# The front of batch 0 in pair order: first keys and queries issued first, small casts and x copies on ScalarE, the sine's table ahead of six of them

## The chip, the cores and the metric

One core of one Trainium2 chip runs the whole program. The metric is device time in microseconds (us), as a median over runs. A core has five engines, each with an instruction queue of its own that is worked through in order: TensorE (PE in the profile, its weight loads PEld), VectorE (DVE), ScalarE (ACT), GpSimd (POOL) and SyncE (SP), which here only issues DMAs. Sixteen DMA engines move data for whichever queue issued the transfer. An instruction that must wait for another engine or for a DMA waits on a semaphore, and everything behind it in its queue waits as well.

## The reference

Two parts in a row: attention in chunks of 32 queries over 56 keys around them and 8 memory keys, then a feed-forward layer with the "snake" activation.

```python
# q, k, v: 4 batches, 8 heads, 768 positions, 64 dims; mem_k, mem_v: 8 rows per head
for c in range(24):
    q_c = q[:, :, 32*c : 32*c+32]
    k_full = concat([mem_k, k[:, :, max(0, 32*c-16) : min(768, 32*c+40)]])
    v_full = concat([mem_v, v[:, :, the same rows]])
    scores = q_c @ k_full.T / 8
    a = exp(scores - max);  a = a / (sum(a) + 1e-9)
    out[:, :, 32*c : 32*c+32] = a @ v_full

x = out as 3072 tokens of 512            # heads side by side
h = x @ w_in                             # 512 x 2048
g = h + sin(alpha * h)**2 / (alpha + 1e-9)
result = g @ w_out                       # 2048 x 512, float32
```

## The kernel before

The kernel works through the four batches one after the other. Attention of a batch gives xT, the layer's input with its 512 columns on the partitions; the layer is then computed in 16 tiles of 128 hidden units ("b" and "h" are the two halves of a tile's first product, followed by the sine on ScalarE; "q" squares it, "g" finishes the tile) and a second product with w_out. While a batch's layer runs on TensorE, the attention of the next batch is worked in between. For batch 0 there is nothing to work it into: everything until the first tile's sine is the *front*, and it is the part that the change touches.

The order of the work is written out by hand. `WORDS` holds one string per stage; `Stage.run` takes it word by word, and a word such as `a4A` calls `do_a("4A")`, which issues the instructions. Each engine gets its instructions in the order of these words. The words of the front:

- `aNE` (L691, L693): casts float32 data to bf16; N is 0 to 3 for the keys of head pair 0 to 3 (k0 to k3), 4 to 7 for the queries (q0 to q3); E is the engine, V for VectorE, A for ScalarE. Pair 3 comes through GpSimd (`dq068`, `dk068`), whose DMAs cast.
- `kN`, `lN` (L313): TensorE turns keys or queries of pair N by 12 transposes. `KNE` (L324), `LNE` (L333): the engine E puts the turned keys into kT, the queries into qT.
- `sNH` (L351, L359, L366): mask and scores of pair N, half H, and their exponential on ScalarE. `vNH` (L378, L387, L388): product with the values on TensorE, then reciprocal and product on VectorE ("normalisation", out comes x_blk).
- `tNH`, `TNH` (L400, L403): TensorE transposes x_blk, and VectorE (t) or ScalarE (T) copies it into xT.
- `Ck` (L812 to L820): memory keys cast, turned and, by `put_memk` (L244), spread into kT of batch 0 and of batch 1. `Cf` (L827) casts the memory values, `m0` (L225) spreads them into vw. `Cl` makes alpha, `Cb`, `Cm`, `Ci` the mask.
- `p0`, `P0` (L462): the first three of the four terms of tile 0's halves, those of the pairs in EARLY. `We`, `Ws` (L743): a one-element activation that makes ScalarE load the table of exp or of sin.
- `yN`, `zN` (L730, L724): matmuls of zeros that keep TensorE busy. `V024` and its like: loads of values of batch 0 by GpSimd (heads 2 and 3 here). `dm`, `I02`, `I27`: memory values of the other batches and w_in by GpSimd.

The float loads of k and q (`load_f`, L753) are issued ahead of all words, keys on SP's queue, queries on ScalarE's own. The eight hardware semaphores DMAHW0 to DMAHW7 are given to these DMAs in turn; a DMA that takes a semaphore for the second time first waits until the earlier DMA on it has landed. PSUM has eight banks; scores, values and a tile take two, a turn or an x transpose takes one, and `Banks` hands them out as the program is built.

Of the kernel before, what the change touches and what calls it, by code (L numbers as in the profile page):

```python
# [11 lines left out]
NEG = -30000.0  # L12
CROSSED = {0: (0, 0), 1: (0, 0), 2: (1, 1), 3: (1, 1)}
KW = 1024
EARLY = (0, 1, 3)
BF = mybir.dt.bfloat16
F32 = mybir.dt.float32
ACTF = mybir.ActivationFunctionType
# [2 lines left out]

WORDS = (
    (
# [4 lines left out]
    ),  # L28
    (
# [93 lines left out]
def kernel(  # L123
# [12 lines left out]
    nc = tc.nc  # L136
    B, H, S, D = q.shape
    NM = mem_k.shape[2]
# [3 lines left out]
    HP = H // 2  # L142
# [31 lines left out]
    memv_st = consts.tile([P, B, H, D], BF, name="memv_st")  # L174
# [4 lines left out]
    NK = NM * sum(not CROSSED[b][0] for b in range(B))  # L179
    memk_bf = memv_st[0:NK, 0]  # L180
# [43 lines left out]
    def put_memv(b, eng=None):  # L224
        (eng or nc.vector.tensor_copy)(  # L225
            vws[b % 2][64:72, :, :, 0:D],
            memv_st[64:72, b, :, :].unsqueeze(2).to_broadcast([NM, H, NJ, D]),
        )

    def put_memv_heads(b):  # L230
        for h in range(H):
            nc.gpsimd.tensor_copy(
                vws[b % 2][64:72, h, :, 0:D],
                memv_st[64:72, b, h, :].unsqueeze(1).to_broadcast([NM, NJ, D]),
            )
# [7 lines left out]
    def put_memk(b):  # L243
        nc.vector.tensor_copy(  # L244
            kTs[b % 2][:, :, 24:856].rearrange("p g (j c) -> p g j c", c=104)[:, :, :, 40:40 + NM],
            memkT[:, :, NM * b:NM * b + NM].unsqueeze(2).to_broadcast([P, HP, NJ, NM]),
        )
# [208 lines left out]
    def half_tile(t, hf, kts=range(KT)):  # L456
        done = t["done"][hf]
        for kt in kts:
            if kt in done:
                continue  # L460
            done.append(kt)
            nc.tensor.matmul(  # L462
                t["hT"][:, hf, 0:HALF],
                w_in_sb[:, kt, P * t["ft"]:P * t["ft"] + P],
                t["xT"][:, kt, HALF * hf:HALF * hf + HALF],
                start=(len(done) == 1), stop=(len(done) == KT),
            )

    def opened(ft, xT):
        hT, bs = banks.pair()  # L470
        return {"ft": ft, "xT": xT, "hT": hT, "bs": bs, "done": [[], []]}
# [69 lines left out]
    class Stage:  # L541
# [29 lines left out]
        def early(self, a, hf):  # L571
            if int(a) not in self.tile:
                self.tile[int(a)] = opened(int(a), self.next_x() if self.i < 0 else self.xT)
            half_tile(self.tile[int(a)], hf, EARLY if self.i < 0 else range(3))

# [101 lines left out]
        def do_m(self, a):  # L677
            put_memv(int(a))

        def do_H(self, a):  # L680
            put_memv_heads(int(a))

# [64 lines left out]
    kq_f = [mlp.tile([P, 2, 6 * D], F32, name="kq_f", tag=t) for t in ("u", "s2") * 4]  # L747
    memk_f = mlp.tile([P, H, D], F32, name="memk_f", tag="o_sb", bufs=3)
    memv_f = mlp.tile([P, H, D], F32, name="memv_f", tag="o_sb", bufs=3)
    alpha_rows = mlp.tile([FT, P], F32, name="alpha_rows", tag="o_sb", bufs=3)  # L750

    def load_f(ring, src, hp, t):
        ring.dma_start(  # L753
            t[:], src[0, 2 * hp:2 * hp + 2].rearrange("h (p r) d -> p h (r d)", p=P)
        )

    for bb in range(B):
        if not CROSSED[bb][0]:
            nc.scalar.dma_start(memk_f[NM * bb:NM * bb + NM], mem_k[bb].rearrange("h n d -> n h d"))
    nc.sync.dma_start(alpha_rows[:], moe_alpha.rearrange("(ft p) -> ft p", p=P))  # L760
    for hp in range(HP - 1):
        load_f(nc.sync, k, hp, kq_f[hp])
        load_f(nc.scalar, q, hp, kq_f[4 + hp])
        if hp == 0:
            nc.sync.dma_start(memv_f[64:72], mem_v[0].rearrange("h n d -> n h d"))
    nc.vector.memset(zeros[:], 0.0)
    nc.vector.memset(tiny[:], 0.0)
    nc.vector.memset(mcol[:], 0.0)
# [33 lines left out]
    def const_i():  # L802
# [5 lines left out]
        nc.gpsimd.tensor_copy(mind[:, 0, 0, :], asum[:, 5:6].to_broadcast([P, 32]))  # L808
        nc.gpsimd.tensor_copy(mind[:, NJ - 1, 2, :], asum[:, 6:7].to_broadcast([P, 32]))

    def const_k():
        nc.vector.tensor_copy(memk_bf, memk_f[0:NK])  # L812
        bank, bs = banks.single()
        mt = bank[:, 0:2 * NK].bitcast(BF).rearrange("p (g c) -> p g c", g=HP)
        for g in range(HP):
            nc.tensor.transpose(
                mt[:, g, :], memk_bf[:, 2 * g:2 * g + 2, :].rearrange("p e d -> p (e d)"),
                ident[0:NK, 0:NK]
            )
        nc.vector.tensor_copy(memkT[:], mt)  # L820
        put_memk(0)
        if not CROSSED[1][0]:
            put_memk(1)
        banks.give(bs)

    def const_f():
        nc.vector.tensor_copy(memv_st[64:72, 0], memv_f[64:72])  # L827

    def const_l():
        nc.vector.tensor_copy(ident_f[:], ident[0:FT, 0:FT])  # L830
# [20 lines left out]
    def const_s():  # L851
        nc.gpsimd.memset(kst[0:32, 0, :], 0.0)
        nc.gpsimd.memset(kst[96:128, NJ - 1, :], 0.0)

    consts_of = dict(b=const_b, f=const_f, m=const_m, i=const_i, k=const_k, l=const_l, p=const_p, v=const_v,
                     s=const_s, z=const_z)

    first = {}
# [35 lines left out]
```

## Time and profile before

| what | us |
| --- | --- |
| median of 3 runs | 215.82 |
| lowest, highest run | 214.7, 217.43 |
| span of the profiled execution | 212.0 |
| TensorE busy in that span | 203.1 |
| VectorE, ScalarE, GpSimd busy | 139.9, 142.8, 100.8 |

The runs are timed from outside, the span runs from the first to the last instruction of one profiled execution; the median lies 3.8 above the span. The execution has no time of its own beside its span.

In the rows below, a timeline row is: start in us from the span's start, us taken, engine, source line, operation, out<-in with the shape, how many were merged, and in brackets the idle time before it with what ended it. A row of the chain of waits is start, us, and what held the chain. ACTq and SPq are the issuing of DMAs by those queues. A row of the windows view is a stretch, its length, the busy time (and count) of PE, PEld, DVE, ACT and POOL, the granted TensorE clock, the mean share of the DMA engines, and GB/s.

### The profile page before, as it was taken

What the parts mean: (1) busy time and instruction counts of PE and PEld (TensorE: products, weight loads), DVE (VectorE), ACT (ScalarE), POOL (GpSimd) and SP (SyncE); (2) the same over time, 40 slices, a digit from 0 to 9 for tenths busy, and PEclk for the clock granted to TensorE, in tenths of its full rate; (3) what the DMA queues carried; (4) which work ended last, traced back from release to release, by engine and by line L of the source; (5) the groups of instructions that cost most, each with busy time, mean ns of one, the idle gap of its engine ahead of it and who ended that gap; (6) DMA issues with size and microseconds to landing.
All of it is one profiled execution on the core that took longest, in us unless ns stands there. A gap on an engine that the chain in (4) does not pass through costs nothing.

```text
span 212.0 us, 4567 instructions
## 1 busy us (share of the span) xinstructions
PE 203.1 (96%) x1759; PEld 117.6 (55%) x1781; DVE 139.9 (66%) x211; ACT 142.8 (67%) x228; POOL 100.8 (48%) x142
## 2 busy tenths in 40 slices
PE   7798899999999999999999999999999999999994
PEld 7566555655455555555456555554555555554443
DVE  4788788999352669957675659887347189964011
ACT  2698798978838479978827299878755188891110
POOL 8988607498696395119894048960000023300000
PEclk9999999999999999999999999999999999999999
DMA  5999999999999999999998259999244400000312
GB/s 163 327 156 145 209 208 204 204 164 177 151 167 128 172 128 128 103 148 147 158 186 137 68 126 125 160 173 126 103 105 108 136 0 3 2 0 0 152 49 99
DMA packets 95853, 27.82 MB, mean 131 GB/s; under 512 B 84808, under 2 KB 92376, under 8 KB 95832
## 3 DMA queue, kind: packets, MB, share of 16 engines
q0 software_dynamic: 69152, 13.64, 85.9%
q1 hardware_dynamic: 25720, 12.68, 30.3%
q10 hardware_dynamic: 960, 1.21, 1.7%
q8 instruction: 14, 0.23, 0.5%
q14 instruction: 7, 0.06, 0.1%
HBM read 29.66 MB, written 6.29 MB: 170 GB/s over the span
## 4 chain that ended last, share of the span: by engine, by line
PE 77%; DVE 8%; ACT 5%; issue 4%; DMA 3%; POOL 1%; SPq 1%; DVEq 0%
PE ps L500 39%; PE ps L462 28%; DVE gT L489 3%; DMA kq_f<-in_k_dram 3%; PE ps L448 3%; DVE s L485 3%; PE ps L419 2%; ACT u L477 2%; DVE x_blk L388 2%; PE ps L313 1%; PE ps L400 1%; ACT qT L333 1%; POOL s L485 1%; ACT s L482 1%; PE ps L359 1%
## 5 line engine op out<-in xcount | busy, mean ns | idle before, releaser
L500 PE MATMUL ps<-w_out_sb,gT 128*128 128x512 bf16 (+2 forms) x382 | 86.9, 370 | 1.3 <-issue 0.3
L462 PE MATMUL ps<-xT,w_in_sb 128*128 128x384 bf16 x512 | 86.4, 326 | 0.6 <-DVE gT L489 0.3
L489 DVE SCALAR_TENSOR_TENSOR gT<-s,inv_alpha,ps 128x768 bf16<-128x768 f32 x64 | 63.1, 1012 | 11.9 <-POOL s L485 5.3
L462 PEld LDWEIGHTS <-w_in_sb 128*128 128x128 bf16 x512 | 49.6, 98 | 35.5 <-issue 2.3
L477 ACT ACTIVATE u<-ps,alpha_sb 128x768 f32<-128x768 f32 x64 | 56.6, 894 | 18.2 <-PE ps L462 17.9
L500 PEld LDWEIGHTS <-gT 128*128 128x128 bf16 x400 | 36.6, 98 | 37.8 <-DVE gT L489 0.2
L485 POOL TENSOR_TENSOR s<-u 128x768 f32<-128x768 f32 x11 | 17.9, 1632 | 65.5 <-ACT u L477 54.5
L433 ACT ACTIVATE pt<-ps,biasm 128x256 bf16<-128x256 f32 x72 | 27.1, 488 | 10.5 <-PE ps L419 10.5
L507 DVE COPY o_sb<-ps 128x512 f32<-128x512 f32 (+1 forms) x15 | 10.1, 678 | 28.4 <-PE ps L500 26.5
L485 DVE TENSOR_TENSOR s<-u 128x768 f32<-128x768 f32 x24 | 22.9, 953 | 7.3 <-ACT u L477 7.3
L482 ACT ACTIVATE s<-u 128x768 f32<-128x768 f32 x29 | 24.2, 841 | 0.5
L388 DVE TENSOR_TENSOR x_blk<-ps,rinv 96x512 bf16<-96x512 f32 x32 | 22.0, 687 | 1.1
L507 ACT COPY o_sb<-ps 128x512 f32<-128x512 f32 (+1 forms) x10 | 5.6, 561 | 22.3 <-PE ps L500 22.3
L387 DVE RECIPROCAL rinv<-ps 96x8 f32<-96x8 f32 x32 | 6.4, 199 | 13.4 <-PE ps L448 12.7
L209 POOL DMA_DIRECT2D vw<-in_v_dram x13 | 11.9, 912 | 6.6 <-PE ps L400 5.5
L216 POOL DMA_DIRECT2D vw<-in_v_dram x13 | 13.3, 1024 | 3.3 <-DMA vw<-in_v_dram 3.0
L275 POOL DMA_DIRECT2D kst<-in_k_dram x16 | 12.1, 758 | 1.7 <-DMA vw<-in_v_dram 0.9
L269 POOL DMA_DIRECT2D kst<-in_k_dram x16 | 11.7, 731 | 1.9 <-DMA vw<-in_v_dram 1.2
L282 POOL DMA_DIRECT2D q_bf<-in_q_dram x12 | 10.7, 911 | 0.0
L448 PEld LDWEIGHTS <-pt 128*128 128x128 bf16 x192 | 8.2, 97 | 4.2 <-ACT pt L433 0.3
L403 ACT COPY xT<-ps 128x384 bf16<-128x384 bf16 x10 | 4.9, 496 | 7.7 <-PE ps L400 7.7
L448 PE MATMUL ps<-vw,pt 128*128 128x65 bf16 x192 | 8.9, 193 | 0.0
(83 smaller groups left out, 139.0 us busy)
## 6 DMA issues: line engine op xcount, KB each, us to landing
out_dram<-o_sb SPq DMA_DIRECT2D x23, 256.0 KB, 2.7
q_bf<-in_q_dram POOLq DMA_DIRECT2D x12, 128.0 KB, 7.0
kq_f<-in_k_dram SPq DMA_DIRECT2D x3, 384.0 KB, 6.0
kq_f<-in_q_dram ACTq DMA_DIRECT2D x3, 384.0 KB, 8.5
w_in_sb<-in_moe_w_in_dram POOLq DMA_DIRECT2D x1, 1152.0 KB, 12.6
vw<-in_v_dram POOLq DMA_DIRECT2D x7, 128.0 KB, 7.8
vw<-in_v_dram POOLq DMA_DIRECT2D x8, 112.0 KB, 8.0
kst<-in_k_dram POOLq DMA_DIRECT2D x14, 64.0 KB, 5.9
```

What stands on the lines that cost most here:

```text
L216: nc.gpsimd.dma_start(vw[72:128, c0:hi, 0:D], win(vflat, base + QW * c0 + 48, hi - c0, 56))
L275: nc.gpsimd.dma_start(kst[72:72 + n, j, :].rearrange("p (h d) -> p h d", d=D), k[b, :, QW * j + 48:QW * j + 48 + n, :].rearrange("h p d -> ...
L388: nc.vector.tensor_tensor(out=x_blk[:].rearrange("p g e d -> p e g d"), in0=otv[0:QW, :, :, 0:D], in1=rinv[:].unsqueeze(3).to_broadcast([Q ...
L433: nc.scalar.activation(pt[:, 0:H * QW].rearrange("p (g e c) -> p g e c", g=2, e=4)[:, :, :, 32 * m:32 * m + 32], sc[:, :, 0:4 * QW].rearra ...
L448: nc.tensor.matmul(otv[:, e, hp, :], pt[:, QW * i:QW * i + P], vws[b % 2][:, 2 * hp + e, j, 0:D + 1],)
L462: nc.tensor.matmul(t["hT"][:, hf, 0:HALF], w_in_sb[:, kt, P * t["ft"]:P * t["ft"] + P], t["xT"][:, kt, HALF * hf:HALF * hf + HALF], start= ...
L477: nc.scalar.activation(t["u"][:], t["hT"][:, :, 0:HALF], ACTF.Sin, scale=alpha_sb[:, ft:ft + 1])
L482: nc.scalar.activation(s2[:], u[:], ACTF.Square)
L485: e.tensor_tensor(out=s2[:], in0=u[:], in1=u[:], op=ALU.mult)
L489: nc.vector.scalar_tensor_tensor(out=gT[:, ft, :].rearrange("p (e c) -> p e c", e=2), in0=t["s2"][:], scalar=inv_alpha[:, ft:ft + 1], in1= ...
L500: nc.tensor.matmul(o[:, c0:c1], gT[:, ft, P * s:P * s + P], w_out_sb[:, ft, c0:c1], start=(ft == 0), stop=(ft == FT - 1),)
L507: copier(state["engines"][state["o"] % len(state["engines"])])(o_sb[:, c0:c1], o[:, c0:c1])
```

## The change

Six things change, all in batch 0's front but the last:

1. The first loads: k0 and q0 are issued before the memory keys, alpha and the memory values, and the memory keys move from ScalarE's queue to SP's.
2. `WORDS[0]` is rewritten: the pairs are taken in the order 0, 1, 2, 3; `We` stands ahead of the first cast.
3. k0 and k1 are cast on VectorE and q1 on ScalarE; all four puts of keys are VectorE's, all four of queries ScalarE's.
4. The casts of memory keys (a new word `Cc`) and memory values go from VectorE to ScalarE.
5. All eight x copies are ScalarE's; `Ws` stands behind the eighth exponential and T01, ahead of the other six copies. EARLY becomes pairs 0, 1, 2.
6. The spread of the memory keys for batch 1 leaves `Ck` and becomes the word `n1` in the next stage, behind `h0`.

```diff
-EARLY = (0, 1, 3)
+EARLY = (0, 1, 2)
...
-        'y1 y1 y1 Ci y1 a4A We y1 Cb a1A y1 y2 y1 y1 dq068 Cl y1 Cm y1 Cf z1 z1 eVA z1 eVA a0A Ck m0 Cz z1 '
...
+        'y1 y1 y1 Ci y1 We y1 Cb a4A y1 y2 y1 y1 dq068 Cl y1 Cm a0V y1 Cc z1 z1 eVA l0 L0A k0 K0V Ck Cz dk068 z1 '
...
-        'o8 b0 h0 I7g q0V U69 U12 b1 h1 dq108 q1A b4 h4 b3 g0 h3 b6 g1 dk108 q4V g4 q3A b2 h2 h6 b5 h5 Ufg g3 '
+        'o8 b0 h0 n1 I7g q0V U69 U12 b1 h1 dq108 q1A b4 h4 b3 g0 h3 b6 g1 dk108 q4V g4 q3A b2 h2 h6 b5 h5 Ufg g3 '
...
+        def do_n(self, a):
+            put_memk(int(a))
...
+    load_f(nc.sync, k, 0, kq_f[0])
+    load_f(nc.scalar, q, 0, kq_f[HP])
     for bb in range(B):
         if not CROSSED[bb][0]:
-            nc.scalar.dma_start(memk_f[NM * bb:NM * bb + NM], mem_k[bb].rearrange("h n d -> n h d"))
+            nc.sync.dma_start(memk_f[NM * bb:NM * bb + NM], mem_k[bb].rearrange("h n d -> n h d"))
     nc.sync.dma_start(alpha_rows[:], moe_alpha.rearrange("(ft p) -> ft p", p=P))
-    for hp in range(HP - 1):
+    nc.sync.dma_start(memv_f[64:72], mem_v[0].rearrange("h n d -> n h d"))
+    for hp in range(1, HP - 1):
         load_f(nc.sync, k, hp, kq_f[hp])
-        load_f(nc.scalar, q, hp, kq_f[4 + hp])
-        if hp == 0:
-            nc.sync.dma_start(memv_f[64:72], mem_v[0].rearrange("h n d -> n h d"))
+        load_f(nc.scalar, q, hp, kq_f[HP + hp])
...
+    def const_c():
+        nc.scalar.copy(memk_bf, memk_f[0:NK])
+
     def const_k():
-        nc.vector.tensor_copy(memk_bf, memk_f[0:NK])
...
         put_memk(0)
-        if not CROSSED[1][0]:
-            put_memk(1)
...
     def const_f():
-        nc.vector.tensor_copy(memv_st[64:72, 0], memv_f[64:72])
+        nc.scalar.copy(memv_st[64:72, 0], memv_f[64:72])
```

Below is what stands in a row on an engine at the places that matter, first before and then in the changed kernel (its line numbers are 1 or 2 off those of before). The text in brackets names the semaphores waited for: DMAHW0 to 7 of the DMAs, otherwise the engine. ScalarE at the program's start, before (kq_f holds the float data, tiny is the one-element activation):

```order
L759 DMA memk_f<-in_mem_k_dram 8x8x64 x2
L753 DMA kq_f<-in_q_dram 128x2x384 x2
L753 DMA kq_f<-in_q_dram 128x2x384 [waits DMAHW1_49]
L693 ACT_TABLE_LOAD
L693 CAST q_bf<-kq_f 128x768 [waits DMAHW5_49]
L743 ACTIVATE tiny<-zeros 1x1 [waits DVE_49]
```

The same place in the changed kernel:

```order
L755 DMA kq_f<-in_q_dram 128x2x384 x2
L755 DMA kq_f<-in_q_dram 128x2x384 [waits DMAHW1_49]
L745 ACT_TABLE_LOAD
L745 ACTIVATE tiny<-zeros 1x1 [waits DVE_49]
L695 CAST q_bf<-kq_f 128x768
L815 CAST memv_st<-memk_f 16x512 [waits DMAHW3_49,DMAHW2_49]
L332 COPY qT_86<-ps 128x768 [waits PE_49]
```

The third load of queries waits for DMAHW1 in both. Before, that was alpha's semaphore, and the cast of q0 waits for another (DMAHW5); in the changed kernel it is q0's own, so that the cast has nothing left to wait for. The table load stands behind that issue in both. On SP the third load of keys waits for DMAHW0, which was the memory keys' and is now k0's.

VectorE between the mask (mrow) and the first normalisation, before:

```order
L799 COPY mrow<-ps 128x128 [waits PE_49]
L827 CAST memv_st<-memv_f 8x512 [waits DMAHW4_49]
L812 CAST memv_st<-memk_f 16x512 [waits DMAHW3_49,DMAHW0_49]
L820 COPY memkT<-ps 128x64 [waits PE_49]
L244 COPY kT_84<-memkT 128x4x8x8 [waits DVE_49]
L244 COPY kT_85<-memkT 128x4x8x8
L225 COPY vw_88<-memv_st 8x64x64
L691 TENSOR_TENSOR q_bf<-kq_f 128x768 [waits DMAHW7_49]
L691 TENSOR_TENSOR k_bf<-kq_f 128x768 [waits DMAHW0_49]
L691 TENSOR_TENSOR q_bf<-kq_f 128x768 [waits DMAHW1_49]
L324 COPY kT_84<-ps 128x8x2x48 [waits PE_49,Activation_49]
L324 COPY kT_84<-ps 128x8x2x48 [waits PE_49]
```

The same place in the changed kernel:

```order
L802 COPY mrow<-ps 128x128 [waits PE_49]
L693 TENSOR_TENSOR k_bf<-kq_f 128x768 [waits DMAHW0_49]
L323 COPY kT_84<-ps 128x8x2x48 [waits PE_49]
L825 COPY memkT<-ps 128x64 [waits PE_49]
L243 COPY kT_84<-memkT 128x4x8x8 [waits DVE_49]
L693 TENSOR_TENSOR k_bf<-kq_f 128x768 [waits DMAHW6_49]
L693 TENSOR_TENSOR q_bf<-kq_f 128x768 [waits DMAHW1_49]
L323 COPY kT_84<-ps 128x8x2x48 [waits PE_49]
L693 TENSOR_TENSOR k_bf<-kq_f 128x768 [waits DMAHW0_49]
L224 COPY vw_88<-memv_st 8x64x64 [waits Activation_49]
L323 COPY kT_84<-ps 128x8x2x48 [waits PE_49]
L323 COPY kT_84<-ps 128x8x2x48 [waits PE_49,Activation_49]
```

The casts are now, in this order, k0, k1, q2 and k2, with the puts of k0 and k1 between them; the spread of the memory values (L224) comes behind the casts and no longer ahead of them.

ScalarE around the sine's table, before:

```order
L366 ACTIVATE pt_102<-ps 128x768 [waits PE_49]
L366 ACTIVATE pt_103<-ps 128x768 [waits DVE_49,PE_49]
L403 COPY xT<-ps 128x384 [waits PE_49] x3
L743 ACT_TABLE_LOAD
L743 ACTIVATE tiny<-zeros 1x1 [waits Activation_49]
L477 ACTIVATE u<-ps,alpha_sb 128x768 [waits PE_49]
```

and in the changed kernel:

```order
L365 ACTIVATE pt_103<-ps 128x768 [waits DVE_49,PE_49]
L402 COPY xT<-ps 128x384 [waits PE_49]
L745 ACT_TABLE_LOAD
L745 ACTIVATE tiny<-zeros 1x1 [waits Activation_49]
L402 COPY xT<-ps 128x384 [waits DVE_49,PE_49]
L402 COPY xT<-ps 128x384 [waits PE_49] x3
L402 COPY xT<-ps 128x384 [waits DVE_49,PE_49]
L402 COPY xT<-ps 128x384 [waits PE_49]
L476 ACTIVATE u<-ps,alpha_sb 128x768 [waits DMAHW0_49,PE_49]
```

Six copies of x now stand between the table load and the first sine (u); before there were none on this engine.

More of the change, by code (lines that the diff above doesn't have):

```diff
@@ L853, in const_s @@
         nc.gpsimd.memset(kst[96:128, NJ - 1, :], 0.0)
-    consts_of = dict(b=const_b, f=const_f, m=const_m, i=const_i, k=const_k, l=const_l, p=const_p, v=const_v,
+    consts_of = dict(b=const_b, c=const_c, f=const_f, m=const_m, i=const_i, k=const_k, l=const_l, p=const_p, v=const_v,
                      s=const_s, z=const_z)
```

5 rows, old and new, of the table WORDS are left out of this document.

## The prediction

> **What bounds the kernel now.** I read the page's busy table first, then its slices:
>
> ```profile
> PE 203.1 (96%) x1759; PEld 117.6 (55%) x1781; DVE 139.9 (66%) x211; ACT 142.8 (67%) x228; POOL 100.8 (48%) x142
> PE   7798899999999999999999999999999999999994
> ```
>
> TensorE is the bound of the kernel as a whole. Only the first slices (5.3 us each) stand under 9, and this is the front, where batch 0's attention runs before any dense work is ready. TensorE's own timeline shows where that ends:
>
> ```profile
> 11.15 0.34 PE L359 MATMUL ps<-qT,kT 64*128 64x96 bf16 x8 [0.30 <-ACT kT L324]
> ...
> 24.17 10.18 PE L462 MATMUL ps<-xT,w_in_sb 128*128 128x384 bf16 x61
> ```
>
> The first scores run at 11.15; from 24.17 on TensorE works through dense matmuls with hardly a gap. The diff rewrites the front and adds one word behind it, so the change is worth the shift of that point, carried to the end one for one. Next the chain of waits, inside the first 40 us, tells what sets the point:
>
> ```profile
> 2.13 5.95 DMA kq_f<-in_k_dram
> ...
> 8.11 1.09 ACT k_bf L693 x2
> ...
> 10.37 0.73 ACT kT L324
> ...
> 22.41 0.70 DVE x_blk L388
> ...
> 25.18 0.91 ACT u L477
> ```
>
> A load, ScalarE's casts and copies, then VectorE's normalisations, then the first sine at 25.18. I use that sine as the end of the front. VectorE's timeline carries most terms:
>
> ```profile
> 8.62 0.72 DVE L244 COPY kT<-memkT 128x256 bf16<-128x256 bf16 x2
> 9.36 1.22 DVE L225 COPY vw<-memv_st 8x4096 bf16<-8x4096 bf16 x1
> 10.61 0.96 DVE L691 TENSOR_TENSOR q_bf<-kq_f 128x768 bf16<-128x768 f32 x1
> 11.49 0.95 DVE L691 TENSOR_TENSOR k_bf<-kq_f 128x768 bf16<-128x768 f32 x1
> ...
> 13.72 0.96 DVE L324 COPY kT<-ps 128x768 bf16<-128x768 bf16 x1 [0.42 <-PE ps L313]
> 14.97 0.96 DVE L324 COPY kT<-ps 128x768 bf16<-128x768 bf16 x1 [0.29 <-PE ps L313]
> ...
> 17.25 0.20 DVE L387 RECIPROCAL rinv<-ps 96x8 f32<-96x8 f32 x1 [0.49 <-ACT qT L333]
> ...
> 18.44 0.20 DVE L387 RECIPROCAL rinv<-ps 96x8 f32<-96x8 f32 x1 [0.26 <-ACT pt L366]
> ...
> 22.18 0.20 DVE L387 RECIPROCAL rinv<-ps 96x8 f32<-96x8 f32 x1
> ...
> 23.02 0.19 DVE L387 RECIPROCAL rinv<-ps 96x8 f32<-96x8 f32 x1
> 23.24 0.69 DVE L388 TENSOR_TENSOR x_blk<-ps,rinv 96x512 bf16<-96x512 f32 x1
> 23.85 0.88 DVE L403 COPY xT<-ps 128x384 bf16<-128x384 bf16 x3
> 26.12 0.96 DVE L485 TENSOR_TENSOR s<-u 128x768 f32<-128x768 f32 x1 [1.39 <-ACT u L477]
> ```
>
> From 10.61 to the end of the last normalisation at 23.24 + 0.69 = 23.93, VectorE waits only 0.42 + 0.29 + 0.49 + 0.26 = 1.46. It is the front's narrow place. Behind another operation a cast costs 0.88 (10.61 to 11.49), a put of keys (L324) about the same, and a reciprocal with its product 0.84 (22.18 to 23.02).
>
> **The start on ScalarE.** Its timeline, the starts of the three query loads in the list of that tile, and the DMA's share and rate:
>
> ```profile
> 1.69 1.46 ACTq L753 DMA_DIRECT2D kq_f<-in_q_dram  x3
> 3.18 1.28 ACT L693 ACT_TABLE_LOAD   x1 [3.18 <-DMA alpha_rows<-in_moe_alpha_dram]
> 6.74 0.83 ACT L693 CAST q_bf<-kq_f 128x768 bf16<-128x768 f32 x1 [2.28 <-DMA kq_f<-in_q_dram]
> 7.48 0.20 ACT L743 ACTIVATE tiny<-zeros 1x1 f32<-1x1 bf16 x1
> ```
>
> ```profile
> L753 ACTq DMA_DIRECT2D kq_f<-in_q_dram x3: 388/412/506, 1.7 to 2.8; - x3
> DMA to landing us min/median/max: 6.0/7.6/9.4
> ```
>
> ```profile
> 2.00:4.00 2.00, 2.00 (x22) 2.00 (x20) 1.49 (x10) 0.82 (x1) 1.83 (x6) 1.00 0.68 196
> 4.00:6.00 2.00, 2.00 (x20) 1.77 (x18) 0.10 (x1) 0.46 (x1) 2.00 (x13) 1.00 1.07 345
> 10.00:12.00 2.00, 1.65 (x31) 1.07 (x27) 1.97 (x3) 1.56 (x3) 1.83 (x2) 1.00 1.51 208
> ```
>
> Before, the third query load waits for alpha's semaphore only (hence the release at 3.18), and the table is loaded long before q0 (pair 0's queries) lands at 6.74. In the changed order the same slot is shared with q0: the third issue waits until q0 has landed, and the table load, which stands behind that issue, loses its cover. On SP the third key load likewise waits for k0, with nothing else queued behind it for a long time.
>
> q0 flew 6.74 - 1.69 = 5.05; issued at 0.75, it lands at 5.8 by that row. The other end: 196 GB/s over two us and then 345 move the 0.79 MB of k0 and q0 by 5.1, and about 0.46, one issue, earlier now, so 4.7. I take 5.6, near the measured flight. Then one issue of 0.49 (1.46 for three), the table 1.28, the tiny activation 0.20 and the cast 0.83: 8.4, where it was 6.74 + 0.83 = 7.57. The early issue gains about 1.1 at the landing; the uncovered issue, table and activation take back 2.0.
>
> The Trainium skill (ScalarE: Activation LUTs, "What ACT_TABLE_LOAD costs") gives 1283 ns for the load and a drain of about 1380 ns on top. This trace agrees with the first (1.28) and has no row of the second; with it the cast would end near 9.8 (estimate from that page).
>
> **From the cast to the first scores.** On TensorE q0 and k0 are turned one behind the other; on VectorE the keys are put (0.96) and then the memory keys:
>
> ```profile
> 8.40 0.19 DVE L820 COPY memkT<-ps 128x64 bf16<-128x64 bf16 x1 [0.35 <-PE ps L816]
> ```
>
> ```profile
> 8.61 0.53 PE L313 MATMUL ps<-ident,q_bf 128*64 128x128 bf16 x12
> ```
>
> Two turns at up to 0.53 give 9.4, the put 10.4, memkT 0.19 and one spread of 0.36 (half of 0.72) 10.95. First scores at 11.0 against 11.15: the new order by itself wins 0.15. The cast of k0 on VectorE (0.95) lies in the idle time before this, and so do ScalarE's small casts, of memory keys and values, in its gaps.
>
> **VectorE from there to its last normalisation.** Left to do at 10.95: casts of k1, q2, k2 (3 x 0.88), puts of k1, k2, k3 (3 x 0.88), the memory values 1.22, eight normalisations (8 x 0.84 = 6.7): 13.2, some 13.3 with the last one's full length. Before, from 10.61: 23.93 - 10.61 - 1.46 = 11.9. The difference is put k1 (0.88) and the memory values, which used to stand ahead of 10.61 (1.22), less the one x copy that stood between normalisations (about 0.3) and rounding. So the x copies taken off VectorE buy little here: three of its four came behind the last normalisation already (the 0.88 at 23.85), where they bounded nothing else on that engine.
>
> Waits: the second in this row is the cast of q2. It was the last of the float loads to land, at most 2.8 + 9.4 = 12.2, and VectorE is ready for it at 10.95 + 0.88 = 11.83: 0.37. Its issue is held back from 2.8 to 5.6, but the 16 engines are busy with the loads ahead of it (share 1.07 and 1.51 in the rows above), so I keep 12.2 and leave a later landing to a rival. k2 is cast two operations later, at about 14, and has 1.7 us more to come. TensorE's order between pairs stood for 0.26 to 0.49 a time before; I count one, 0.35. Together 10.95 + 13.3 + 0.7 = 24.95, against 23.93.
>
> **The tail.** Before, 25.18 - 23.93 = 1.25 from the last product to the sine. Now the last x goes through ScalarE:
>
> ```profile
> 18.33 0.47 ACT L403 COPY xT<-ps 128x384 bf16<-128x384 bf16 x1
> ...
> 22.91 1.28 ACT L743 ACT_TABLE_LOAD   x1
> ```
>
> The sine's table falls behind the eighth exponential and ahead of six x copies (6 x 0.47 = 2.8), so these run late. TensorE takes the first three terms of tile 0's halves between the last transposes and stands in line for these copies; I put 0.3 on top: 1.55. The sine starts at 24.95 + 1.55 = 26.5, **1.3 later**.
>
> **Behind the front.** The word n1 (one spread, 0.36) falls on VectorE's 1.39 of idle time at 26.12 and costs nothing; without that cover, 0.36. The weights were no limit at 24.17 and a later start only helps. GpSimd's loads of values go out in pair order, three of them 0.6 sooner:
>
> ```profile
> 5.61 0.57 POOL L845 MEMSET pt<- 128x32 bf16 x8
> ...
> 14.18 0.87 POOL L216 DMA_DIRECT2D vw<-in_v_dram  x1
> ```
>
> ```profile
> vw<-in_v_dram POOLq DMA_DIRECT2D x8, 112.0 KB, 8.0
> ```
>
> The last of them started at 14.18; with a median of 8.0 to landing it arrives by about 22, and pair 3's values are now used last, at about 22.5. I take nothing for it, and up to 0.5 if it is late.
>
> Sum: span 212.0 + 1.3 = 213.3. The median of the runs shown, 215.82, is 3.8 above that span, so **217.1**.
>
> **The rivals.**
> *Late loads (slower).* If k2 and q2, issued 2.7 to 3.3 later than before, keep their flight of up to 9.4, q2 lands at 6.1 + 9.4 = 15.5; VectorE stands before its second cast, and everything behind moves by 3.3: 217.1 + 3.3 = 220.4, past the 2% mark. It decides from a landing above 12.2, one for one. For it: the issue order itself. Against: q2's flight before was queueing behind two other query loads. The Trainium skill (DMA: Bandwidth & Descriptors, "Issuing engines are not separate DMA queues") says that DMAs of all issuers interleave on the same 16 engines; by that the last bytes land when they did, and the gain of issuing k0 and q0 first is only in who is first. Chance of a landing above 13: 0.17, a third of it past 2%.
> *The waits go (faster).* If q0 lands at 4.7, q2 by 11.3 and pair order leaves VectorE no wait, it starts its row near 10.4, ends at 23.7, with the old tail 24.95: 215.6; with 0.5 more from a smoother start of the dense part, 215. Against: it still has 1.4 us more in that row. 0.15.
> *The clock falls.* Fewer filler matmuls run, and TensorE may idle from 9.4 to 11.0 but for the memory keys and a filler. The granted clock is 1.00 in every row above, although TensorE was busy only 1.65 of 2 us at 10 to 12. At half clock each of the six turns that VectorE and ScalarE still wait for takes up to 0.53 longer, some 3 us: 220. 0.03.
> *The change isn't what it says.* The sine's table is early in the order, but its 1.28 only moves from the last x copies to six of them; that is in the forecast.
>
> **The numbers.** Forecast 0.65 (its own range 216 to 218.6: q0's two ends, 0.3 to 0.7 of waits, the tail), late loads 0.17, waits gone 0.15, clock 0.03. The runs before spread from 214.7 to 217.43, so 2% is about what can be told from no change, and the likeliest case lies inside it. Range 214.9 to 219.5. Faster by over 2%: 0.03; slower: 0.09; within: 0.88.
>
> **What would show it.** ScalarE's table load after q0's landing, at 5.5 to 6.5, and its first cast ending at 8 to 8.8; first scores at 11; VectorE waiting for DMA at its q2 cast; last product at 24.5 to 25.5; dense matmuls 1.3 later. I am wrong if the table still runs by 3.5, if q2's cast waits for over 1 us, or if the dense part, the same on both sides here, differs by more than 1 us.

## The result, and the profile after

| | before | changed kernel |
| --- | --- | --- |
| median of 4 runs each, same chip | 215.70 us | 218.69 us |
| lowest, highest | 214.70, 217.43 | 217.21, 218.80 |
| span of the profiled execution | 212.0 | 215.0 |
| first sine in it | 25.18 | 27.42 |

The ratio is 1.0138, 95% interval [1.0094, 1.0181]: slower, by less than 2%. The change cost 3.0 us in the profiled span and in the medians, where the prediction gave 1.3. Each experiment below has its ratio to the kernel before as it ran beside it on one chip (medians there 214.91, 215.52 and 215.19 us), so medians of different experiments are not to be compared directly. A ratio leaves out slow executions, those over 1.5% above the fastest of the same kernel.

The page's busy line and TensorE's slices, after:

```profile
PE 202.5 (94%) x1747; PEld 116.8 (54%) x1766; DVE 139.8 (65%) x208; ACT 143.4 (67%) x231; POOL 101.2 (47%) x142
...
PE   7668799999999999999999999998999999999994
```

The second and third slices (5.3 and 5.4 us each) fell from 7 and 9 tenths to 6 and 6, so the loss begins within the first 16 us. ScalarE's timeline:

```profile
0.75 5.02 ACTq L755 DMA_DIRECT2D kq_f<-in_q_dram  x3
5.80 1.28 ACT L745 ACT_TABLE_LOAD   x1 [5.80 <-DMA kq_f<-in_q_dram]
7.10 0.20 ACT L745 ACTIVATE tiny<-zeros 1x1 f32<-1x1 bf16 x1
7.21 0.81 ACT L695 CAST q_bf<-kq_f 128x768 bf16<-128x768 f32 x1
...
22.38 1.28 ACT L745 ACT_TABLE_LOAD   x1
...
27.42 0.90 ACT L476 ACTIVATE u<-ps,alpha_sb 128x768 f32<-128x768 f32 x1 [0.41 <-PE ps L461]
```

Three issues take from 0.75 to 5.77 (0.75 + 5.02), since the third stands until q0 has landed; only then the table load starts, and q0's cast ends at 8.02. TensorE's timeline:

```profile
1.20 4.45 PE L732 MATMUL ps<-zeros 128*128 128x128 bf16 x40 [1.20 <-DVE tiny L770]
7.44 0.20 PE L836 MATMUL ps<-ident_f,alpha_rows 16*128 16x16 f32 x1 [1.79 <-DMA alpha_rows<-in_moe_alpha_dram]
...
11.24 0.35 PE L358 MATMUL ps<-qT,kT 64*128 64x96 bf16 x8 [0.73 <-DVE kT L243]
...
148.50 0.35 PE L418 MATMUL ps<-qT,kT 64*128 64x96 bf16 x8 [0.90 <-DMA qT<-q_bf]
```

TensorE stands still for 1.79 before alpha, a load that nobody waited for before, and for 0.90 far behind the front, at batch 3's first scores. Before, these two groups of scores stand as one, without a wait:

```profile
145.10 0.57 PE L419 MATMUL ps<-qT,kT 64*128 64x96 bf16 x16
```

VectorE's timeline in the changed kernel:

```profile
7.68 0.17 DVE L837 COPY alpha_sb<-ps 128x16 f32<-128x16 f32 x1 [4.07 <-PE ps L836]
...
9.78 0.96 DVE L323 COPY kT<-ps 128x768 bf16<-128x768 bf16 x1 [0.62 <-PE ps L312]
...
11.01 0.95 DVE L693 TENSOR_TENSOR k_bf<-kq_f 128x768 bf16<-128x768 f32 x1
12.98 0.96 DVE L693 TENSOR_TENSOR q_bf<-kq_f 128x768 bf16<-128x768 f32 x1 [1.02 <-DMA kq_f<-in_q_dram]
...
25.40 0.69 DVE L387 TENSOR_TENSOR x_blk<-ps,rinv 96x512 bf16<-96x512 f32 x1
```

VectorE is ready for its row at 11.01, waits 1.02 for q2 in the second place of the row, and ends the last product at 26.09 (before: 23.93). The chain of waits says it in two rows, and names a third load at its far end:

```profile
0.75 4.63 DMA kq_f<-in_q_dram
5.40 7.57 DMA kq_f<-in_q_dram
...
140.12 8.24 DMA qT<-q_bf
```

q0's flight, then q2's behind it: q2 was issued at 5.40, when q0 had landed, and was there at 12.97. The third row is a query transpose of batch 3. If one compares the starts of the 64 finishing operations on VectorE (L489 before, L488 after), the changed kernel is 1.8 late in the first of them, 2.0 to 2.2 through batch 2 and 3.0 from batch 3 on. So in this execution the 3.0 are 2.1 from the front and 0.9 from that one late transpose.

### The profile page after: what moved, and what is told of

It is laid out like the page before. It is cut to its first block, busy times and chain, and to the rows that moved or that the text cites. A ratio compares the mean times of both kernels' runs of the same rounds, so it can differ in the third digit from the quotient of the medians.

```text
span 215.0 us, 4538 instructions
## 1 busy us (share of the span) xinstructions
PE 202.5 (94%) x1747; PEld 116.8 (54%) x1766; DVE 139.8 (65%) x208; ACT 143.4 (67%) x231; POOL 101.2 (47%) x142
## 4 chain that ended last, share of the span: by engine, by line
PE 67%; DMA 10%; DVE 8%; SPq 7%; issue 3%; ACT 3%; POOL 1%; DVEq 0%; ACTq 0%
PE ps L499 37%; PE ps L461 23%; DMA kq_f<-in_q_dram 6%; SPq L296 5%; DMA qT<-q_bf 4%; PE ps L447 3%; SPq L299 2%; PE ps L418 2%; DVE gT L488 2%; DVE x_blk L387 2%; DVE s L484 1%; PE ps L399 1%; ACT u L476 1%; DVE kT L323 1%; POOL s L484 1%
## 5 line engine op out<-in xcount | busy, mean ns | idle before, releaser
L488 DVE SCALAR_TENSOR_TENSOR gT<-s,inv_alpha,ps 128x768 bf16<-128x768 f32 x64 | 63.2, 1012 | 11.8 <-POOL s L484 5.3
L506 DVE COPY o_sb<-ps 128x512 f32<-128x512 f32 (+1 forms) x15 | 10.1, 678 | 29.0 <-PE ps L499 27.4
L208 POOL DMA_DIRECT2D vw<-in_v_dram x13 | 11.8, 904 | 6.7 <-PE ps L399 5.6
L215 POOL DMA_DIRECT2D vw<-in_v_dram x13 | 12.3, 949 | 1.8 <-DMA vw<-in_v_dram 1.8
L402 ACT COPY xT<-ps 128x384 bf16<-128x384 bf16 x14 | 6.5, 486 | 8.4 <-PE ps L399 8.4
```

Source lines behind the costliest of these rows:

```text
L215: nc.gpsimd.dma_start(vw[72:128, c0:hi, 0:D], win(vflat, base + QW * c0 + 48, hi - c0, 56))
L488: nc.vector.scalar_tensor_tensor(out=gT[:, ft, :].rearrange("p (e c) -> p e c", e=2), in0=t["s2"][:], scalar=inv_alpha[:, ft:ft + 1], in1= ...
L506: copier(state["engines"][state["o"] % len(state["engines"])])(o_sb[:, c0:c1], o[:, c0:c1])
```

## The experiments

The questions: which part of the change carries the front's 2.2 us (the new load order or the new words); what in the load order does it (q2 held back, alpha late, or the table load that lost its cover); and whether the late transpose at 148 belongs to the change. "First sine" is 25.18 before and 27.42 in the changed kernel.

### One part alone

The changed kernel with the loads of before (new words alone):

```diff
-    load_f(nc.sync, k, 0, kq_f[0])
-    load_f(nc.scalar, q, 0, kq_f[HP])
...
-            nc.sync.dma_start(memk_f[...], mem_k[bb]...)
+            nc.scalar.dma_start(memk_f[...], mem_k[bb]...)
...
-    for hp in range(1, HP - 1):
+    for hp in range(HP - 1):
```

> The changed kernel with the order of the first loads put back as before; all words stay. Loads theory (the front lost its time to the loads: alpha late, third loads held until k0 and q0 land, q2 last at VectorE): ScalarE's table load runs near 3, alpha's copy on VectorE at 5.9 instead of 7.7, q2 lands at about 12.1 instead of 13.0, and the first sine is 0.7 to 1.2 us earlier than in the changed kernel's trace (27.42), at about 26.4; total about 1 us under the changed kernel, ratio to before about 1.008. Work theory (VectorE's longer row of casts and puts alone sets the end): the first sine stays within 0.3 us of 27.4 and the ratio near 1.013.

Measured: 216.39 us, ratio 1.0088 [1.0049, 1.0127], span 213.6, first sine 26.87. VectorE's timeline, at q2's cast:

```profile
12.55 0.96 DVE L693 TENSOR_TENSOR q_bf<-kq_f 128x768 bf16<-128x768 f32 x1 [1.93 <-DMA kq_f<-in_q_dram]
```

The new words suffer with the old loads as well: they ask for q2 in the second place of VectorE's row, and with the old loads q2 lands last, at 12.5. Before, q2 was cast in the third place and the wait hardly showed. The first sine is 0.55 earlier than in the changed kernel, which lies between the two theories: the words cost by themselves, and the loads add to it.

The kernel before with the new load block (loads alone, words of before):

```diff
+    load_f(nc.sync, k, 0, kq_f[0])
+    load_f(nc.scalar, q, 0, kq_f[HP])
...
-            nc.scalar.dma_start(memk_f[...], mem_k[bb]...)
+            nc.sync.dma_start(memk_f[...], mem_k[bb]...)
```

> The kernel before with only the new order of the first loads. Loads theory: alpha's copy at 7.7, the table load after q0's landing at about 5.8, VectorE's three casts start near 11.9 instead of 10.61, the first sine at 26.3 to 26.8 instead of 25.18, ratio to before 1.005 to 1.008. Work theory: the first sine within 0.3 us of 25.2, ratio 1.00.

Measured: 217.58 us, ratio 1.0115 [1.0085, 1.0145], span 216.6, first sine 27.63. TensorE's timeline:

```profile
7.67 0.25 PE L834 MATMUL ps<-ident_f,alpha_rows 16*128 16x16 f32 x1 [2.02 <-DMA alpha_rows<-in_moe_alpha_dram]
...
8.79 1.49 PE L724 MATMUL ps<-zeros 128*128 128x512 bf16 x3
...
11.19 0.85 PE L313 MATMUL ps<-ident,q_bf 128*64 128x128 bf16 x12
```

So each part alone is slower, 0.9% and 1.2%, and both together 1.4%: they don't add. A likely reason, not shown by itself, is that both are paid at the same place, the start of VectorE's row. The first sine came later than either theory said. In this execution a turn of 12 took 0.85, which took 0.53 before, and three fillers 1.49: TensorE ran at about half rate until some 13.9, so part of the 2.45 is that and not the loads' landing. The other nine runs have a mean clock of 0.984 to 0.992, so the 1.2% holds lost clock in every run. More on it below.

### q2's cast moved back

The changed kernel, with k2's cast and the put of k1 ahead of q2's cast:

```diff
-        'a5A a1V Cf V002 s00 z1 s01 l1 L1A Cp a6V V024 k1 K1V y1 s10 a2V V046 ...
+        'a5A a1V a2V Cf V002 s00 z1 s01 l1 L1A Cp V024 k1 K1V a6V y1 s10 V046 ...
```

> The changed kernel with VectorE's casts in another order: k1, k2, then the put of k1, then q2, so that no operation stands behind q2's landing. Loads theory: the wait of 1.02 us for q2 goes, the first sine comes 0.6 to 1.0 us earlier than 27.42. Work theory: the wait only moves to a later place (the put of k1, the pairs' order), and the first sine stays within 0.3 us.

Measured: 219.19 us, ratio 1.0146 [1.0067, 1.0224], first sine 29.43. Nothing was won, but the profiled execution can't tell why: TensorE ran at half rate until about 17 in it, and the put of k1 waited 1.67 for TensorE instead of q2's cast for its DMA. Inconclusive on q2.

### The small loads first

The changed kernel with its words, and a load order that keeps k0 and q0 early but gives the third issues an early landing to wait for (alpha's and the first memory keys'):

```diff
+    nc.sync.dma_start(alpha_rows[:], ...)
+    nc.scalar.dma_start(memk_f[0:NM], mem_k[0]...)
     load_f(nc.sync, k, 0, kq_f[0])
     load_f(nc.scalar, q, 0, kq_f[HP])
-    for bb in range(B):
-        if not CROSSED[bb][0]:
-            nc.sync.dma_start(memk_f[...], mem_k[bb]...)
-    nc.sync.dma_start(alpha_rows[:], ...)
+    nc.sync.dma_start(memk_f[NM:2 * NM], mem_k[1]...)
```

> The changed kernel with alpha (SP) and the first memory keys (ScalarE's queue) issued ahead of k0 and q0, so that the third loads wait for these two small ones and not for k0 and q0. Loads theory: table load near 3, third query load issued before 4, alpha's copy at 5.9, q2 landed by 12.2; the first sine 0.7 to 1.3 us earlier than 27.42, much as with the old order. If instead it is the 16 engines' throughput that sets q2's landing (rival within the loads theory), q2 still lands near 13.0 and the first sine gains under 0.4.

Measured: 215.79 us (10 runs), ratio 1.0023 [0.9987, 1.0058], span 213.0. ScalarE's timeline first, then VectorE's:

```profile
2.99 1.28 ACT L745 ACT_TABLE_LOAD   x1 [2.99 <-DMA memk_f<-in_mem_k_dram]
...
25.73 0.90 ACT L476 ACTIVATE u<-ps,alpha_sb 128x768 f32<-128x768 f32 x1 [0.41 <-PE ps L461]
```

```profile
9.50 0.95 DVE L693 TENSOR_TENSOR k_bf<-kq_f 128x768 bf16<-128x768 f32 x1
10.37 0.95 DVE L693 TENSOR_TENSOR q_bf<-kq_f 128x768 bf16<-128x768 f32 x1
...
23.72 0.69 DVE L387 TENSOR_TENSOR x_blk<-ps,rinv 96x512 bf16<-96x512 f32 x1
```

With the same words, the table load is hidden again, the row starts 1.5 earlier (9.50 against 11.01) and q2's cast waits for nothing. The first sine is 1.7 earlier, more than the 0.7 to 1.3 expected. With the new words, the load order carries 1.7 of the front's 2.24; the rest, 0.55, is the new words' longer row on VectorE: it starts 1.1 before that of before (10.61) and ends 0.5 after it (24.41 against 23.93).

### Alpha alone early

Which of the load order's effects is it? Here only alpha's load goes ahead of k0; the third query load is still held, by k0's landing:

```diff
+    nc.sync.dma_start(alpha_rows[:], ...)
     load_f(nc.sync, k, 0, kq_f[0])
...
-    nc.sync.dma_start(alpha_rows[:], ...)
```

> The changed kernel with alpha's load issued ahead of k0 on SP's queue, and nothing else: alpha is early, but the third query load is still held, now to k0's landing (about 5.2). Tells alpha's late landing from q2's. Both: alpha's copy on VectorE at 5 to 6 instead of 7.7, no idle time of TensorE above 0.8 before the first turns. If q2's landing (12.97 in the changed kernel) sets VectorE's row, q2's cast still waits, by 1.0 to 2.0 for what comes earlier ahead of it, and the first sine stays at 26.9 to 27.5 (27.42 in the changed kernel), ratio 1.010 or more. If alpha carried the loss, the first sine falls to 26.3 or below and the ratio to about 1.005.

Measured: 217.76 us, ratio 1.0110 [1.0020, 1.0199], span 216.0. ScalarE's timeline, then VectorE's:

```profile
6.09 1.28 ACT L745 ACT_TABLE_LOAD   x1 [6.09 <-DMA kq_f<-in_k_dram]
...
27.36 0.90 ACT L476 ACTIVATE u<-ps,alpha_sb 128x768 f32<-128x768 f32 x1 [0.41 <-PE ps L461]
```

```profile
5.90 0.18 DVE L837 COPY alpha_sb<-ps 128x16 f32<-128x16 f32 x1 [2.29 <-PE ps L836]
...
9.27 0.96 DVE L323 COPY kT<-ps 128x768 bf16<-128x768 bf16 x1 [1.71 <-PE ps L312]
...
12.79 0.96 DVE L693 TENSOR_TENSOR q_bf<-kq_f 128x768 bf16<-128x768 f32 x1 [1.34 <-DMA kq_f<-in_q_dram]
```

Alpha 1.8 earlier moved the first sine by 0.06. The first put came 0.5 earlier, and q2's wait grew from 1.02 to 1.34 and took most of that back. So alpha's late landing by itself doesn't carry the loss. TensorE still idled 1.28 before the first turns, now for q0's cast, where at most 0.8 was expected. The held third issue is left: it delays the table load and q0's cast, and it delays q2. Two limits remain. The small loads first also put the first memory keys ahead of q0, which this run doesn't, and no run tells q0's late cast from q2's late landing.

### Alpha's work moved back

The changed kernel with its loads, and alpha's transposes (`Cl`) behind k1's cast:

```diff
-... dq068 Cl y1 Cm a0V ...
+... dq068 y1 Cm a0V ...
-        'a5A a1V Cf V002 ...
+        'a5A a1V Cl Cf V002 ...
```

> The changed kernel with the word that turns and copies alpha moved from ahead of the mask to behind the cast of k1, so that neither TensorE nor VectorE waits for alpha early; the loads stay as changed. Cold-clock theory: TensorE idles about 1 us instead of 1.8 before the first turns and is warm in every execution, first sine 27.2 to 27.5 (q2's landing at 13 still sets it), the slower group of times goes, median 0.5 to 1.5 us under the changed kernel. Rival (alpha's wait costs by itself, not by the clock): VectorE's row moves 1.5 us earlier and the sine with it, to about 26.3.

Measured: 218.98 us, ratio 1.0158 [1.0074, 1.0243], span 218.5, first sine 29.79. The expectation that TensorE would not go idle failed: it waits 1.92 for q0's late cast, its clock falls from about 8.3 on, and then it waits 2.12 for VectorE. The first sine fits neither theory. TensorE's timeline:

```profile
8.19 0.82 PE L312 MATMUL ps<-ident,q_bf 128*64 128x128 bf16 x12 [1.92 <-ACT q_bf L695]
...
12.50 0.28 PE L836 MATMUL ps<-ident_f,alpha_rows 16*128 16x16 f32 x1 [2.12 <-DVE ident_f L833]
```

The windows of 2 us (as in the prediction: start:end, length, PE, PEld, DVE, ACT, POOL, clock, DMA share, GB/s):

```profile
6.00:8.00 2.00, 0.27 (x2) 0.00 (x0) 0.74 (x1) 1.99 (x3) 2.00 (x5) 1.00 1.17 259
8.00:10.00 2.00, 1.81 (x29) 1.50 (x29) 0.32 (x1) 1.61 (x4) 2.00 (x10) 0.57 1.13 301
10.00:12.00 2.00, 0.38 (x1) 0.00 (x0) 1.97 (x5) 1.18 (x2) 2.00 (x5) 0.50 1.46 256
...
18.00:20.00 2.00, 1.95 (x58) 1.74 (x55) 1.94 (x3) 2.00 (x4) 2.00 (x3) 0.87 2.96 131
```

The same with k2's cast and the put of k1 ahead of q2's as well:

```diff
-        'a5A a1V Cl Cf V002 s00 z1 s01 l1 L1A Cp a6V V024 k1 K1V y1 s10 a2V V046 ...
+        'a5A a1V Cl a2V Cf V002 s00 z1 s01 l1 L1A Cp V024 k1 K1V a6V y1 s10 V046 ...
```

> As the one before, and in addition VectorE casts k2 and puts k1 ahead of the cast of q2, as in the earlier run that was spoilt by the slow clock. Loads theory: no operation waits for q2, first sine at 26.0 to 26.6, that is 0.8 to 1.4 earlier than with alpha later alone. Work theory: another wait takes its place, within 0.3 us of the one before.

Measured: 218.22 us, ratio 1.0111 [1.0039, 1.0184], span 216.4, first sine 28.74. TensorE's timeline, then the windows:

```profile
8.15 0.53 PE L312 MATMUL ps<-ident,q_bf 128*64 128x128 bf16 x12 [1.81 <-ACT q_bf L695]
...
11.36 0.23 PE L836 MATMUL ps<-ident_f,alpha_rows 16*128 16x16 f32 x1 [1.85 <-DVE ident_f L833]
...
13.32 0.85 PE L312 MATMUL ps<-ident,q_bf 128*64 128x128 bf16 x12
```

```profile
12.00:14.00 2.00, 2.00 (x29) 1.23 (x27) 1.05 (x2) 1.38 (x2) 1.37 (x4) 0.50 2.50 151
14.00:16.00 2.00, 1.75 (x28) 1.15 (x26) 1.14 (x2) 1.02 (x2) 2.00 (x3) 0.69 3.41 145
```

q2's cast waits no more, but the put of k1 waits 1.42 for turns that take 0.85. The first sine is 1.05 earlier than in the run before, but the stretch at half rate is also shorter (3.4 against 10.2), so the gain can't be put down to q2, and 26.0 to 26.6 was far off. In neither run did moving work behind the late loads help: while q0's cast is late, TensorE has nothing to do.

### The words, with good loads

The sine's table, ahead of six x copies or behind all eight (loads as in "the small loads first"):

```diff
-... T00 v10 s31 T01 Ws dm v11 ... p0 T30 P0 T31 '
+... T00 v10 s31 T01 dm v11 ... p0 T30 P0 T31 Ws '
```

> The changed kernel with the small loads first (alpha and the first memory keys, as in the earlier run with a first sine at 25.73) and with the table of the sine loaded behind all eight x copies. If the early table is worth its place: the load (1.28) and the tiny activation stand between the last copy and the sine, where TensorE's last matmuls hide 0.8, and the first sine is 0.5 to 0.9 later, at 26.2 to 26.6. If the six late copies cost as much as the table (my tail of 0.3): within 0.3 of 25.7.

Measured: 216.19 us, ratio 1.0028 [0.9995, 1.0061], span 214.0. ScalarE's timeline:

```profile
26.36 1.66 ACT L476 ACTIVATE u<-ps,alpha_sb 128x768 f32<-128x768 f32 x2
```

The early table is worth 0.63 at the first sine (25.73 against 26.36, one execution of each), as expected, though the medians can't tell the two apart. The words of before with the small loads first (memory keys on SP's queue):

```diff
+    nc.sync.dma_start(alpha_rows[:], ...)
+    nc.sync.dma_start(memk_f[0:NM], mem_k[0]...)
+    load_f(nc.sync, k, 0, kq_f[0])
+    load_f(nc.scalar, q, 0, kq_f[4])
+    nc.sync.dma_start(memk_f[NM:2 * NM], mem_k[1]...)
+    nc.sync.dma_start(memv_f[64:72], mem_v[0]...)
+    for hp in range(1, HP - 1):
```

> The words of before with the new load order's gain and without its harm: alpha and the first memory keys, then k0, second memory keys, memory values, k1, k2 on SP's queue, q0, q1, q2 alone on ScalarE's. Theory (load order was the whole harm; the words of before are as good): alpha's copy on VectorE at 5 to 6, q0's cast ends by 7.6, no wait above 0.5 for a DMA on VectorE before the first normalisation, first sine 25.2 to 26.2, ratio 0.998 to 1.004. Rival (the words of the change are needed for this load order): ScalarE's table load uncovered behind q0 (third issue held), cast of q0 ends 8.0 or later, first sine 26.5 to 27.5, ratio 1.007 or more. If the wait on batch 3's last query transpose belongs to the memory keys on SP's queue, it is here as well (0.4 to 1.8).

Measured: 214.92 us, ratio 1.0020 [0.9980, 1.0059], span 212.8, first sine 25.05. The old words neither win nor lose with these loads. VectorE's row starts no earlier than before (its cast of q1 at 10.79, before at 10.61), and its timeline shows why: it waits 1.50 for the memory values, which now stand behind k0 and the memory keys on SP's queue. No wait above 0.5 was expected.

```profile
7.19 0.42 DVE L827 CAST memv_st<-memv_f 8x512 bf16<-8x512 f32 x1 [1.50 <-DMA memv_f<-in_mem_v_dram]
```

No version beat the kernel before.

### The late transpose of batch 3

A wait of TensorE at batch 3's second group of scores stood in every kernel with memory keys on SP's queue, and in none of two with both on ScalarE's (the kernel before and the loads of before). The changed kernel with small loads first and both on ScalarE's:

```diff
-    nc.sync.dma_start(memk_f[NM:2 * NM], mem_k[1]...)
+    nc.scalar.dma_start(memk_f[NM:2 * NM], mem_k[1]...)
```

> The changed kernel with alpha, first keys, memory values, k1, k2 on SP's queue and both loads of memory keys with q0, q1, q2 on ScalarE's own; words unchanged. Question: the wait of TensorE on batch 3's last query transpose (0.4 to 1.8 us near 148) stood in every kernel in which at least one memory-key load went out on SP's queue, and in none of the two with both on ScalarE's. Theory A (the queue of the memory keys decides it): no wait above 0.12 at batch 3's first scores; front as with the small loads first, first sine 25.5 to 26.2 (one more issue of 0.4 to 0.5 ahead of the table load may cost up to that), span 212.4 to 213.4, ratio 1.000. Theory B (the transposes' flight varies by chance or follows the shift of the front): a wait of 0.3 to 1.0 there again, first sine the same, span 213 to 214, ratio 1.002.

Measured: 216.28 us, ratio 1.0026 [0.9975, 1.0077], span 212.3, first sine 25.74, and no such wait on TensorE's timeline, where the two groups of scores stand as one:

```profile
145.58 0.57 PE L418 MATMUL ps<-qT,kT 64*128 64x96 bf16 x16
```

That spoke for the queue, but the kernel before, profiled again, has it too:

> The kernel before, unedited, profiled a second time. If batch 3's late query transpose is chance, a wait of 0.3 or more on it can stand here too; if it belongs to the memory keys on SP's queue, none above 0.12 is here. First sine 25.0 to 25.5, clock 0.995 or more, span 212 to 212.6.

Measured: span 212.2, first sine 25.01, and on TensorE's timeline:

```profile
145.72 0.35 PE L419 MATMUL ps<-qT,kT 64*128 64x96 bf16 x8 [0.44 <-DMA qT<-q_bf]
```

So the wait is not a mark of the change; its length varies between executions of one kernel (0 and 0.44 before; 0.90 and, in the run below, 0.44 after). Whether a later front makes it longer stays open: the longest ones, 1.3 to 1.8, stood in kernels whose front ended 2.2 to 4.6 late, but the run with a front 4.3 late had 0.89.

The changed kernel, unedited, a second time:

> The changed kernel once more, unedited, for a second trace beside the next ones. Cold-clock theory (TensorE's wait of 1.8 us for alpha falls into its warm-up, and in some executions it then stays at half rate until 13 to 16 us, as in two of the traces so far): the executions fall in two groups about 1.5 us apart; where the trace is of the slower group, its 128x512 fillers near 8.5 start 0.4 us apart instead of 0.2 and the first sine is near 29; in the faster group 27.4. Rival (the clock plays no part in the changed kernel itself): fillers at 0.2 and the first sine at 27.4 in the trace, one group of times.

Measured: 218.14 us, ratio 1.0112 [1.0051, 1.0173], span 215.3, first sine 28.18: the wait before alpha was 2.14, q2's cast started at 13.47 after a wait of 1.16, and the late transpose cost 0.44. The sine fits neither the 27.4 nor the 29 expected, and the four runs lie within 0.8 us and show no two groups. In the trace the turns took 0.53, so the clock is not what made this sine 0.76 later than in the first trace; q0 landed 0.4 later, and all that hangs on it followed. The front's loss thus varies between executions: 2.24 and 3.00 in these two. A first sine that differs by less than 0.8 between two single executions (0.55 and 0.63 above) is no proof alone; the 1.7 of the small loads first is clear of that, and the interval of its ratio (up to 1.0058) lies below the changed kernel's in the first table (from 1.0094).

## Why the prediction was right, and where it was too small

It said 217.1, and no difference that can be told from the runs' spread. 218.69 came: inside the whole range, just above the 216 to 218.6 of its likeliest case, and a slowdown that the interval does tell from none. The direction and the main step (the table load that loses its cover) were right; the loss was more than twice the forecast. By its steps:

- **The table load behind the held issue: right.** Forecast at 5.5 to 6.5, it started at 5.80; q0's cast ended at 8.02 (forecast 8.4). Giving the third issue an early landing to wait for brought the table load back to 2.99.
- **First scores and the start of VectorE's row: right.** 11.24 against 11.0; 11.01 against 10.95. This is luck in part, for two errors cancel. q0's cast ended 0.38 earlier than forecast. But the cast of k0, which the forecast put into VectorE's idle time, stood behind alpha's copy (7.68), so it ran from 8.21 to 9.16, k0's turns began only at 9.21, and the put waited for them. The alpha load was missing from this sum. It landed 5.3 after its issue (before 2.0), because it now stands behind k0 and the memory keys on SP's queue. The Trainium skill (DMA: Bandwidth & Descriptors, "Queues, rings and completion order") has descriptors of one ring consumed in order on each engine, which agrees. With alpha early the first sine was only 0.06 earlier, because q2 was later still.
- **VectorE's row: the terms that were mis-sized are q2's landing and the row's own work.** The prediction kept 12.2, "the 16 engines are busy with the loads ahead of it"; it was 12.97, and the wait 1.02 instead of 0.37. Without the hold, with the small loads first, q2 was there before 10.37 (at 11.42 with both memory keys on ScalarE's queue), so the hold mattered. It isn't all: with the loads of before q2 was not held (issued at 2.87) and still landed at 12.53; there both loads of memory keys stand ahead of the queries on ScalarE's queue. Nor does each us of landing count: q2's cast at 11.42 instead of 10.37 left the first sine where it was (25.74 and 25.73). That is the first rival, late loads, in its small form: above 12.2, from where it was said to decide, and just under 13. The wait also meets one of the prediction's own signs of being wrong, "if q2's cast waits for over 1 us". The forecast's other wait was 0.35 for the order of the pairs; 0.23 is listed. The row's work took 26.09 - 11.01 - 1.25 = 13.8 instead of 13.3. From start to start, the eight normalisations took 7.0 instead of 6.7, the spread of the memory values 1.36 instead of 1.22, the six casts and puts 5.4 instead of 5.3. The prediction's own check had this in it: 11.9 + 0.88 + 1.22 - 0.3 is 13.7, and the 0.4 that it called rounding was most of what its prices left out. Last product: 26.09, forecast 24.95.
- **The tail: a little too long.** 27.42 - 26.09 = 1.33, forecast 1.55. The late x copies did no harm, and the early table helped by 0.63 where it was tried, with the small loads first.
- **n1 costs nothing: right.** Its spread ran at 26.01, in time in which VectorE had nothing else to do until 28.35.
- **The shift carried one for one: right through batch 2**, 2.0 to 2.2 all the way. The 0.9 behind it is the late transpose, which the prediction had called no part of the change; by another of its signs of being wrong, a dense part that differs by over 1 us, it comes just under. That wait also occurs in the kernel before.
- **The clock: given 0.03, and too little.** "The granted clock is 1.00 in every row" was true of one execution. A mean clock below 0.998 stood in four of the eight runs of the changed kernel, in nine of ten with the loads alone and in all eight of the two kernels with alpha's work moved back; in none of 20 of the first two kernels with the small loads first, in three of ten of the third, in one of ten of the words of before with these loads, and in 16 of 57 of before. In the two traces that show a fall, it stands behind TensorE's waits of 1.8 to 1.9 for q0's cast and VectorE (below). But the kernel before falls too in some runs, and once TensorE has started, the longest wait in its front is 0.92 in the trace, so these waits aren't the only cause. The fall wasn't the cause of the 2.2 in the profiled execution, where turns took 0.53.

The sum for the profiled execution: to the forecast shift of 1.3 come 0.65 for q2's landing, 0.53 for the row's work, -0.12 for the other wait, 0.06 for the start and -0.22 for the tail, together 2.2; then 0.9 for the late transpose, less 0.1 of shift absorbed on the way: 3.0.

## What to carry to other kernels

Where DMAs share a few semaphores in turn, moving one load ahead changes what every later issue waits for: list, for the new order, which landing the second use of each semaphore waits for, and what stands behind that issue on its engine. Put small loads in front, so that these waits end early and small data isn't queued behind large. A load that lands last should be used last: the new words asked for q2 second, and VectorE waited 1.93 with the old loads and 1.02 with the new. This last rule is argued from the waits; the two runs that moved q2's cast back lost clock and don't show it.

## What the hardware showed

**TensorE lost its clock after gaps of about 2 us, but not after each.** With 1.81 and 1.85 idle, and little work between, the granted clock went to 0.50 from 11.8 to 15.2. The run's mean clock of 0.992 is the same: 0.008 of 216.4 are 1.7 us of lost full rate, 3.4 us at half. The longer stretch, from 8.3 to 18.5, is 0.977 of 218.5, three times as much. The Trainium skill (TensorE: Matmul & The Clock Gate, "What's actually happening") gives a window of about 3.4 us for both directions; the length of the half-rate stretch agrees with it. Here no single gap ahead of a fall was longer than 1.92, so gaps well below the 3.4 of the stretch, between short bursts, were enough. They don't always do it: behind 1.79 and 2.14 in the two traces of the changed kernel, and behind 2.01 with the words of before and the small loads first, turns took 0.53. What tells the cases apart stays open. Half rate is not free: a turn takes 0.85 instead of 0.53, and VectorE's puts wait for turns.

**The listed clock doesn't show a cold start.** In the loads-alone run every window, 0 to 20, has a clock of 1.00, while three fillers took 1.49 and the turns 0.85. The trace's clock records begin only at 13.87 in this execution (6.37 in the changed kernel's first trace), and the column shows 1.00 where there is no record. The window at its half-rate place:

```profile
10.00:12.00 2.00, 1.83 (x22) 1.10 (x23) 1.58 (x5) 0.00 (x0) 2.00 (x5) 1.00 1.41 264
```

The rate there is read from the duration of a known matmul group, not from the clock column. Whether the alpha wait keeps TensorE cold in such executions was not tried by itself.
